# Attention backward on one core: a new written-out order of loads, stores and units, copies moved between ScalarE and VectorE

## The chip, the cores and the metric

The kernel runs on one core of a Trainium2 chip. The metric is the device time of one launch in microseconds; the median of eleven runs before the change is 672.09 us (670.6 to 673.2).

## What is computed

The reference is a grouped-query softmax attention together with its gradients: 32 batches, 32 query heads that share 4 key and value heads, 4 query rows per head, 2048 keys, depth 128, all bfloat16.

```python
B, Hq, Hkv, Sq, Sk, D = 32, 32, 4, 4, 2048, 128
k = jnp.repeat(k, Hq // Hkv, axis=1)
v = jnp.repeat(v, Hq // Hkv, axis=1)
p = softmax(einsum("bhqd,bhkd->bhqk", q, k) * D ** -0.5)
out = einsum("bhqk,bhkd->bhqd", p, v)
# returned: out, and the gradients dq, dk, dv for a given grad_out
```

For one batch there are 4 key heads with 8 x 4 = 32 query rows each, so the 128 query rows fill the 128 partitions exactly. K and V of a batch are 4 MB and are read once; dK and dV of a batch are 4 MB and are written once.

## The kernel before, in words

Nothing is looped over in the usual sense. The string PLAN (line 28) is cut into pieces of four characters, each piece a unit of work: its kind, its part, a PSUM bank or slot or engine, and a tile number. `plan()` (line 149) turns it into a list of 3232 units, and the loop at line 323 emits them in that order inside a manual schedule. An engine executes its instructions in the order in which they were emitted, so PLAN sets the order on each engine and on SyncE, which issues every DMA. What binds different engines to each other are the data, the PSUM banks and the SBUF tiles that are used again.

The units, by the names that `emit` (line 214 on) uses:

- LK and LV load half of a batch's K or V, two heads, as one row of 8192 bytes per partition in one of 20 slots (`slots`, line 189). The K rows carry q or grad_out as 256 further bytes. The DMA is issued on SyncE at line 226. For batch 0 each load is cut in two at column 2048.
- KT and VT transpose K and V on TensorE, four blocks of 128x128 in fp32 pairs (line 241); KTe, VTe copy them from PSUM to SBUF, on ScalarE (line 207) or on VectorE (line 209) by the letter A or D in the plan. QT and QTe do the same for q and grad_out (line 230 and lines 207 or 209), ET and DT for the probabilities and for dS.
- S is Q K^T in PSUM (line 255), MX the row minimum on VectorE (line 260), EX the exponential on ScalarE (line 264), RC the reciprocal of the sum (line 268). DP is dO V^T (line 255 too) and DS the product for the softmax gradient on VectorE (line 303).
- dop, qp and rs are scalings on GpSimd (lines 271 to 278). O and DQ are the products with V and K (line 288), Oe and DQe their scaled copies (line 294 on ScalarE, line 296 on VectorE), which go into the last 128 columns of an output row.
- DV and DK compute one quarter of the keys for two heads, into two PSUM banks (line 310); DVe and DKe copy these 128x1024 numbers as bfloat16 into an output row (line 316), on ScalarE or VectorE. `heads_of` (line 212) splits the row in two heads, so that a copy writes two pieces of 512.
- SV and SK store a finished output row of dV or dK (line 320).

Loads and outputs share the 20 slots. A load into a slot that held an output row waits until that row's store has landed; a load into a slot that held K or V waits for the last reader. DMAs use eight semaphores in turn, and each waits until the DMA eight places ahead of it has landed, so at most eight are in flight. In the middle of the plan every batch issues in the order LV1, LK0, SK1, SV1, LV0, SV0, LK1, SK0, with each load belonging to a batch three or four later than the one in work. `unpaired` (line 332) puts the output columns into the reference's order on the host; it is not part of the time.

Of the kernel before, what the change touches and what calls it, by code (L numbers as in the profile page):

```python
# [14 lines left out]
P = 128  # L15
# [6 lines left out]

NAMES = dict(
# [5 lines left out]
    "a000a110b120a030b040a150e400f4A0e011f0A0e702f7A0e513f5A0b160a070e224f2A0e135f1D0c000d0D0e316f3A0g720h7A0e637f6A0"  # L29
    "b080a190g601h6D0g212h2A0i040i1-0j0D0g303h3A0e411f4A0e024f0A0g104h1D0k0A0g415h4D0g026h0D0l0D0e705f7A0e516p020q0A0"  # L30
    "f5D0b1a0p131q1D0m0-0A340B3A0A060B0D0A100B1A0a0d0r020r1-0s0D0t0D0o0-0A640B6A0A760B7D0u020v0D0g502h5A0A540B5A0E1c0"
    "b0e0A460B4A0e210f2D0e102f1D0c020d0D0e333f3A0A240B2A0E0b0u160v1D0g703h7A0e617f6A0n0-0C020D0D0C140D1A0C360D3D0a1h0"
    "g604h6A0g216h2A0i021i1-0j0D0C200D2A0g360h3A0e470f4A0w100x1A0k0A0g111h1D0g462h4D0g075h0D0C400D4D0w061x0A0l0D0e072"
    "f0A0C620D6A0F0f0C740D7D0e763f7A0e504p010q0A0f5D0b1i0p171q1D0m0-0A320B3A0A040B0D0A100B1A0a040r060r1-0s0D0t0D0A720"
    "B7D0o0-0A640B6A0u061v0D0g500h5A0y010C540D5A0y1-0z0D0F1g0A520B5A0E120b0c0A460e201f2A0B4D0e115f1D0c040d0D0e356f3A0"
    "A220B2A0E0j0u160v1D0g701h7A0e617f6A0n0-0C040D0D0C120D1A0C360D3D0a180g605h6A0g216h2A0i020i1-0j0D0C200D2A0g360h3A0"
    "e471f4A0w101x1A0g112h1D0k0A0g463h4D0g074h0D0C400D4D0w060x0A0l0D0e072f0A0C620D6A0F060C740D7D0e765f7A0e506p010q0A0"
    "f5D0b100p171q1D0m0-0A320B3A0A040B0D0A100B1A0a0g0r060r1-0s0D0t0D0o0-0A620B6A0A740B7D0y070C500D5A0y1-0z0D0F1b0u020"
    "v0D0g560h5A0A540B5A0E1f0b020A400B4D0e270f2A0e163f1A0c020d0D0e334f3D0A240B2A0E010u100v1D0g722h7A0e637f6A0n0-0C060"
    "D0D0C140D1A0C300D3D0a130g624h6A0g236h2A0i041i1-0j0D0C220D2A0g300h3A0C720e410f4A0w100x1A0g111h1D0k0A0g403h4D0g015"  # L40
    "h0D0C440D4A0w001x0D0l0D0D7A0e012f0D0C660D6A0F0a0e743f7D0e504p020q0A0f5D0b150p111q1D0m0-0A340B3A0A060B0D0A120B1A0"
    "a0b0r000r1-0s0D0t0D0o0-0A640B6A0A760B7D0y010C520D5A0y1-0z0D0F1j0u041v0D0g500h5A0A560B5A0E160b0f0A420B4D0e211f2A0"
    "e105f1A0c040d0D0e356f3D0A260B2A0E0e0u120v1D0g711h7A0e607f6A0n0-0C040D0D0C160D1A0C320D3D0a170g615h6A0g206h2A0i040"
    "i1-0j0D0C200D2A0g320h3A0e431f4A0w101x1A0g112h1D0k0A0g423h4D0g034h0D0C400D4D0w020x0A0l0D0e032f0A0C640D6A0F0i0C760"
    "D7D0e725f7A0e506p010q0A0f5D0b190p131q1D0m0-0A340B3A0A060B0D0A100B1A0a0j0r020r1-0s0D0t0D0o0-0A640B6A0A760B7D0y030"
    "C500D5A0y1-0z0D0F110u040v0D0g520h5A0A560B5A0E1a0b060A400B4D0e230f2A0e123f1A0c040d0D0e354f3D0A260B2A0E0c0u100v1D0"
    "g732h7A0e627f6A0n0-0C040D0D0C160D1A0C300D3D0a1h0g634h6A0g226h2A0i041i1-0j0D0C220D2A0g300h3A0e410f4A0w120x1A0g131"
    "h1D0k0A0g403h4D0g015h0D0C420D4D0w001x0A0l0D0e012f0A0C640D6A0F000C760D7D0e703f7A0e514p020q0A0f5D0b1e0p131q1D0m0-0"
    "A340B3A0A060B0D0A100B1A0a010r020r1-0s0D0t0D0o0-0A640B6A0A760B7D0y030C500D5A0y1-0z0D0F1d0u041v0D0g520h5A0A560B5A0"
    "E1i0b0a0A400B4D0e231f2A0e125f1A0c040d0D0e356f3D0A260B2A0E020u100v1D0g731h7A0e627f6A0n0-0C040D0D0C160D1A0C300D3D0"  # L50
    "a180g635h6A0g226h2A0i040i1-0j0D0C220D2A0g300h3A0e411f4A0w121x1A0g132h1D0k0A0g403h4D0g014h0D0C420D4D0w000x0A0l0D0"
    "e012f0A0C640D6A0F050C760D7D0e705f7A0e516p020q0A0f5D0b1f0p131q1D0m0-0A340B3A0A060B0D0A100B1A0a0d0r020r1-0s0D0t0D0"
    "o0-0A640B6A0A760B7D0y030C500D5A0y1-0z0D0F140u040v0D0g520h5A0A560B5A0E100b090A400B4D0e230f2A0e123f1A0c040d0D0e354"
    "f3D0A260B2A0E0c0u100v1D0g732h7A0e627f6A0n0-0C040D0D0C160D1A0C300D3D0a1g0g634h6A0g226h2A0i041i1-0j0D0C220D2A0g300"
    "h3A0e410f4A0w120x1A0g131h1D0k0A0g403h4D0g015h0D0C420D4D0w001x0A0l0D0e012f0A0C640D6A0F0i0C760D7D0e703f7A0e514p020"
    "q0A0f5D0b160p131q1D0m0-0A340B3A0A060B0D0A100B1A0a040r020r1-0s0D0t0D0o0-0A640B6A0A760B7D0y030C500D5A0y1-0z0D0F130"
    "u041v0D0g520h5A0A560B5A0E150b0e0A400B4D0e231f2A0e125f1A0c040d0D0e356f3D0A260B2A0E020u100v1D0g731h7A0e627f6A0n0-0"
    "C040D0D0C160D1A0C300D3D0a1b0g635h6A0g226h2A0i040i1-0j0D0C220D2A0g300h3A0e411f4A0w121x1A0g132h1D0k0A0g403h4D0g014"
    "h0D0C420D4D0w000x0A0l0D0e012f0A0C640D6A0F000C760D7D0e705f7A0e516p020q0A0f5D0b1a0p131q1D0m0-0A340B3A0A060B0D0A100"
    "B1A0a030r020r1-0s0D0t0D0o0-0A640B6A0A760B7D0y030C500D5A0y1-0z0D0F170u040v0D0g520h5A0A560B5A0E1i0b0f0A400B4D0e230"  # L60
    "f2A0e123f1A0c040d0D0e354f3D0A260B2A0E0c0u100v1D0g732h7A0e627f6A0n0-0C040D0D0C160D1A0C300D3D0a190g634h6A0g226h2A0"
    "i041i1-0j0D0C220D2A0g300h3A0e410f4A0w120x1A0g131h1D0k0A0g403h4D0g015h0D0C420D4D0w001x0A0l0D0e012f0A0C640D6A0F0h0"
    "C760D7D0e703f7A0e514p020q0A0f5D0b150p131q1D0m0-0A340B3A0A060B0D0A100B1A0a070r020r1-0s0D0t0D0o0-0A640B6A0A760B7D0"
    "y030C500D5A0y1-0z0D0F1j0u041v0D0g520h5A0A560B5A0E100b060A400B4D0e231f2A0e125f1A0c040d0D0e356f3D0A260B2A0E020u100"
    "v1D0g731h7A0e627f6A0n0-0C040D0D0C160D1A0C300D3D0a1e0g635h6A0g226h2A0i040i1-0j0D0C220D2A0g300h3A0e411f4A0w121x1A0"
    "g132h1D0k0A0g403h4D0g014h0D0C420D4D0w000x0A0l0D0e012f0A0C640D6A0F010C760D7D0e705f7A0e516p020q0A0f5D0b1i0p131q1D0"
    "m0-0A340B3A0A060B0D0A100B1A0a0j0r020r1-0s0D0t0D0o0-0A640B6A0A760B7D0y030C500D5A0y1-0z0D0F180u040v0D0g520h5A0A560"
    "B5A0E1h0b0a0A400B4D0e230f2A0e123f1A0c040d0D0e354f3D0A260B2A0E0c0u100v1D0g732h7A0e627f6A0n0-0C040D0D0C160D1A0C300"
    "D3D0a1f0g634h6A0g226h2A0i041i1-0j0D0C220D2A0g300h3A0e410f4A0w120x1A0g131h1D0k0A0g403h4D0g015h0D0C420D4D0w001x0A0"
    "l0D0e012f0A0C640D6A0F0d0C760D7D0e703f7A0e514p020q0A0f5D0b100p131q1D0m0-0A340B3A0A060B0D0A100B1A0a080r020r1-0s0D0"  # L70
    "t0D0o0-0A640B6A0A760B7D0y030C500D5A0y1-0z0D0F1g0u041v0D0g520h5A0A560B5A0E110b050A400B4D0e231f2A0e125f1A0c040d0D0"
    "e356f3D0A260B2A0E020u100v1D0g731h7A0e627f6A0n0-0C040D0D0C160D1A0C300D3D0a160g635h6A0g226h2A0i040i1-0j0D0C220D2A0"
    "g300h3A0e411f4A0w121x1A0g132h1D0k0A0g403h4D0g014h0D0C420D4D0w000x0A0l0D0e012f0A0C640D6A0F040C760D7D0e705f7A0e516"
    "p020q0A0f5D0b1h0p131q1D0m0-0A340B3A0A060B0D0A100B1A0a0g0r020r1-0s0D0t0D0o0-0A640B6A0A760B7D0y030C500D5A0y1-0z0D0"
    "F1b0u040v0D0g520h5A0A560B5A0E1d0b0i0A400B4D0e230f2A0e123f1A0c040d0D0e354f3D0A260B2A0E0c0u100v1D0g732h7A0e627f6A0"
    "n0-0C040D0D0C160D1A0C300D3D0a1a0g634h6A0g226h2A0i041i1-0j0D0C220D2A0g300h3A0e410f4A0w120x1A0g131h1D0k0A0g403h4D0"
    "g015h0D0C420D4D0w001x0A0l0D0e012f0A0C640D6A0F030C760D7D0e703f7A0e514p020q0A0f5D0b110p131q1D0m0-0A340B3A0A060B0D0"
    "A100B1A0a0b0r020r1-0s0D0t0D0o0-0A640B6A0A760B7D0y030C500D5A0y1-0z0D0F190u041v0D0g520h5A0A560B5A0E140b000A400B4D0"
    "e231f2A0e125f1A0c040d0D0e356f3D0A260B2A0E020u100v1D0g731h7A0e627f6A0n0-0C040D0D0C160D1A0C300D3D0a150g635h6A0g226"
    "h2A0i040i1-0j0D0C220D2A0g300h3A0e411f4A0w121x1A0g132h1D0k0A0g403h4D0g014h0D0C420D4D0w000x0A0l0D0e012f0A0C640D6A0"  # L80
    "F070C760D7D0e705f7A0e516p020q0A0f5D0b1d0p131q1D0m0-0A340B3A0A060B0D0A100B1A0a090r020r1-0s0D0t0D0o0-0A640B6A0A760"
    "B7D0y030C500D5A0y1-0z0D0F1e0u040v0D0g520h5A0A560B5A0E130b0h0A400B4D0e230f2A0e123f1A0c040d0D0e354f3D0A260B2A0E0c0"
    "u100v1D0g732h7A0e627f6A0n0-0C040D0D0C160D1A0C300D3D0a1i0g634h6A0g226h2A0i041i1-0j0D0C220D2A0g300h3A0e410f4A0w120"
    "x1A0g131h1D0k0A0g403h4D0g015h0D0C420D4D0w001x0A0l0D0e012f0A0C640D6A0F0f0C760D7D0e703f7A0e514p020q0A0f5D0b140p131"
# [64 lines left out]
def plan():  # L149
    text, seen, units = "".join(PLAN), collections.Counter(), []  # L150
    for at in range(0, len(text), 4):
        key = text[at:at + 2]
        u = Unit()
        u.name, u.part, u.b = NAMES[key[0]], int(key[1]), seen[key]
        u.where, u.tile = text[at + 2], int(text[at + 3], 36)
        seen[key] += 1
        units.append(u)
# [3 lines left out]
def kernel(  # L161
# [160 lines left out]
    with tc.manual_schedule():  # L322
        for u in units:
            emit(u)
# [37 lines left out]
```

## Time and profile before

| | before |
|---|---|
| median of 11 runs, us | 672.09 |
| the profiled execution's own time, us | 672.05 |
| its span, us | 670.1 |
| mean granted TensorE clock | 0.986 |
| PE busy, us | 606.2 |
| VectorE busy, us | 571.8 |
| ScalarE busy, us | 569.4 |
| bytes moved by DMA, MB | 273.96 |
| mean rate over the span, GB/s | 409 |
| output copies of line 316: on ScalarE | 292 of 1023 ns |
| output copies of line 316: on VectorE | 220 of 1218 ns |
| copies of transposes: on ScalarE | 445 of about 600 ns (512 fp32 words wide) |
| copies of transposes: on VectorE | 195 of about 685 ns |
| median time from a load's or store's issue to its landing, us | 17.8 to 20.5 |

The span runs from the first to the last instruction of the profiled execution; its own time has 1.95 us more around it. A page of the profile divides the span in 40 slices and gives for each the busy share of the engines in tenths, the mean busy share of the 16 DMA engines, and the rate. A busy share is an average over stages: a wait matters only where it ends last. Three engines and the DMA queue are all busy for 85% of the span or more, so the reading has to go stretch by stretch.

### The profile page before, as it was taken

Reading aid. Unit: us, or ns where it says so; the run is one execution under the profiler, and the core shown is the slowest. Engines: PE = TensorE matmul, PEld = TensorE weight load, DVE = VectorE, ACT = ScalarE, POOL = GpSimd, SP = SyncE. Lnnn points to the kernel's source line nnn. Section 1 sums busy time; section 2 is a strip of 40 time slices with the busy share of each in tenths; the row PEclk is TensorE's granted clock in tenths of the full one; section 3 lists DMA queues with packets and bytes.
Section 4 is the critical chain, followed back from the end, with each engine's and each line's share of the span. In section 5 each row is a group of like instructions: output and inputs, shape, how many; then the busy total and the mean of one; then the engine's idle time right before and its main releaser. Section 6 shows DMA issues by size and latency. Waiting matters only on the chain.

```text
span 670.1 us, 20678 instructions
## 1 busy us (share of the span) xinstructions
PE 606.2 (90%) x8768; PEld 399.4 (60%) x8768; DVE 571.8 (85%) x736; ACT 569.4 (85%) x802; POOL 39.0 (6%) x102
## 2 busy tenths in 40 slices
PE   5998999999998999988998989888999988898994
PEld 5665666666665666655666656555565665565652
DVE  1988799999997999988898889887988988887893
ACT  3997899999997899988898889887888988887894
POOL 0000000000000000000000000000000000000000
PEclk9999899999998999999999999998999999999997
DMA  8999999999999999999999999999999999999967
GB/s 347 421 424 422 418 376 423 423 423 424 423 424 425 424 425 422 423 427 426 422 422 407 408 414 423 423 426 416 393 421 416 421 421 408 410 421 425 375 245 314
DMA packets 37532, 273.96 MB, mean 409 GB/s; under 512 B 4160, under 2 KB 4160, under 8 KB 5184
## 3 DMA queue, kind: packets, MB, share of 16 engines
q1 hardware_dynamic: 37440, 272.65, 98.2%
q8 instruction: 68, 1.11, 0.6%
q14 instruction: 24, 0.20, 0.1%
HBM read 136.31 MB, written 136.31 MB: 407 GB/s over the span
## 4 chain that ended last, share of the span: by engine, by line
DMA 47%; PE 40%; ACT 4%; DVE 4%; issue 3%; SPq 0%; POOL 0%; DVEq 0%; ACTq 0%; POOLq 0%
DMA row<-in_k_dram 47%; PE psum L241 20%; PE psum L310 9%; PE psum L288 6%; PE psum L255 5%; ACT row L316 3%; DVE vt_sb L209 3%; DVE ds_sb L303 1%; DVE row L316 0%; ACT e_sb L264 0%; DVE e_sb L260 0%; PE psum L230 0%; ACT dt_sb L207 0%; SPq L226 0%; DVE row L296 0%
## 5 line engine op out<-in xcount | busy, mean ns | idle before, releaser
L316 ACT CAST row<-psum 128x1024 bf16<-128x1024 f32 x292 | 289.2, 1023 | 30.8 <-PE psum L310 28.5
L241 PE MATMUL psum<-ident,row 128*128 128x128 f32 x2048 | 287.6, 282 | 30.1 <-DMA row<-in_k_dram 23.9
L241 PEld LDWEIGHTS psum<-ident,row 128*128 128x128 f32 x2048 | 222.7, 142 | 96.7 <-issue 30.6
L316 DVE CAST row<-psum 128x1024 bf16<-128x1024 f32 x220 | 264.9, 1218 | 5.6 <-PE psum L310 2.6
L207 ACT COPY kt_sb<-psum 128x512 f32<-128x512 f32 x190 | 110.1, 599 | 22.3 <-PE psum L241 22.2
L207 ACT COPY vt_sb<-psum 128x512 f32<-128x512 f32 x160 | 92.0, 602 | 34.1 <-PE psum L241 33.5
L303 DVE SCALAR_TENSOR_TENSOR ds_sb<-psum,delta,e_sb 128x1024 bf16<-128x1024 f32 x64 | 82.1, 1283 | 12.9 <-PE psum L255 8.3
L310 PE MATMUL psum<-ds_sb,qp_sb 32*128 32x512 bf16 x512 | 77.3, 385 | 3.4 <-ACT row L316 1.0
L260 DVE TENSOR_SCALAR_CACHE_REDUCE e_sb<-psum 128x2048 bf16<-128x2048 f32 x32 | 73.3, 2292 | 5.7 <-PE psum L255 5.7
L310 PE MATMUL psum<-e_sb,dop_sb 32*128 32x512 bf16 x512 | 68.4, 387 | 2.4 <-issue 0.9
L209 DVE COPY vt_sb<-psum 128x1024 bf16<-128x1024 bf16 x96 | 60.7, 685 | 10.1 <-PE psum L241 9.9
L209 DVE COPY kt_sb<-psum 128x1024 bf16<-128x1024 bf16 x66 | 45.0, 684 | 28.6 <-PE psum L241 27.8
L264 ACT ACTIVATE e_sb<-psum,m 128x2048 bf16<-128x2048 f32 x32 | 64.0, 2001 | 0.2 <-DVE e_sb L260 0.2
L271 POOL TENSOR_SCALAR dop_sb<-row,rinv 128x128 bf16<-128x128 bf16 x32 | 19.3, 603 | 603.4 <-DVE rinv L268 585.2
L241 PE MATMUL psum<-ident,ds_sb 128*128 128x128 f32 x256 | 42.2, 288 | 9.6 <-DVE vt_sb L209 7.0
L288 PE MATMUL psum<-row,dt_sb 128*32 128x128 bf16 x2048 | 44.0, 224 | 5.4 <-issue 5.3
L310 PEld LDWEIGHTS <-qp_sb 32*128 32x128 bf16 x512 | 19.4, 91 | 46.3 <-issue 42.9
L255 PE MATMUL psum<-vt_sb,qdt_sb 128*32 128x512 bf16 x512 | 40.7, 388 | 4.3 <-issue 4.3
L288 PEld LDWEIGHTS <-dt_sb 128*32 128x32 bf16 x2048 | 31.2, 96 | 21.6 <-issue 20.9
L241 PEld LDWEIGHTS psum<-ident,ds_sb 128*128 128x128 f32 x256 | 27.1, 141 | 27.2 <-DVE vt_sb L209 16.4
L207 ACT COPY dt_sb<-psum 128x512 f32<-128x512 f32 x63 | 38.4, 610 | 1.0 <-PE psum L241 0.9
L288 PEld LDWEIGHTS <-et_sb 128*32 128x32 bf16 x2048 | 31.0, 96 | 13.8 <-ACT et_sb L207 11.3
(29 smaller groups left out, 308.5 us busy)
## 6 DMA issues: line engine op xcount, KB each, us to landing
out_dram<-row SPq DMA_DIRECT2D x64, 1056.0 KB, 20.0
out_dram<-row SPq DMA_DIRECT2D x64, 1024.0 KB, 20.4
row<-in_k_dram SPq DMA_DIRECT2D x62, 1056.0 KB, 17.8
row<-in_v_dram SPq DMA_DIRECT2D x62, 1024.0 KB, 20.5
row<-in_v_dram SPq DMA_DIRECT2D x4, 512.0 KB, 9.8
row<-in_k_dram SPq DMA_DIRECT2D x2, 544.0 KB, 5.6
row<-in_k_dram SPq DMA_DIRECT2D x2, 512.0 KB, 4.4
```

What stands on the lines that cost most here:

```text
L207: nc.scalar.copy(out=out.bitcast(FP32), in_=in_)
L209: nc.vector.tensor_copy(out=out, in_=in_.bitcast(BF16))
L241: nc.tensor.transpose(out=ps[:, P * j:P * j + P], in_=src[:, 4 * half + j, :], identity=ident32[:])
L255: nc.tensor.matmul(out[r, QW * w:QW * w + QW], lhsT=t["qdt"][:, P * side + 32 * h:P * side + 32 * h + 32], rhs=t[x, NH * i + h][:, QW * w: ...
L260: nc.vector.tensor_scalar(out=t["e"][:], in0=t["S"], scalar1=-scale, scalar2=None, op0=ALU.mult, op1=ALU.min, accum_out=t["m"][:])
L264: nc.scalar.activation(out=t["e"][:], in_=t["S"], func=ACT.Exp, bias=t["m"][:], scale=scale, accum_out=t["l"][:])
L271: nc.gpsimd.tensor_scalar(out=t["dop"][:], in0=t["go"], scalar1=t["rinv"][:], scalar2=None, op0=ALU.mult)
L288: nc.tensor.matmul(t[name][r, :], lhsT=left[:, j, r, odd], rhs=right[:, 4 * i + j, :, odd], start=(i == 0 and c == 0), stop=(i == 1 and c ...
L303: nc.vector.scalar_tensor_tensor(out=t["ds"][:, w], in0=t["DP", i], scalar=t["dl"][:], in1=t["e"][:, w], op0=ALU.subtract, op1=ALU.mult)
L310: nc.tensor.matmul(acc[:, QW * (h % 2):QW * (h % 2) + QW], lhsT=t[still][rows[h], :], rhs=t[moving][rows[h], QW * i:QW * i + QW], start=Tr ...
L316: copy(out=heads_of(t[name[:2], "out", g])[:, :, QW * i:QW * i + QW], in_=t[name[:2], i, g].rearrange("p (h c) -> p h c", h=2))
```

## The change

PLAN is replaced as a whole: 3236 units instead of 3232. The bytes moved and the matrix products are the same. What is different in the order and in the code:

- In the middle of the plan the four loads of a batch stand together, ahead of the stores SK0 of the previous batch and SV0, SV1, SK1. The first twelve loads stand ahead of the first store. In the last five batches loads and stores are mixed irregularly.
- Units on TensorE stand at other places relative to each other and use other PSUM banks.
- Copies change their engine. On ScalarE there are now 345 output copies (from 292), 314 copies of transposes (from 445), 30 of the 32 copies QTe (from none) and 30 of the 64 scaled copies Oe and DQe (from none); VectorE has the rest.
- The loads of batch 0 are no longer cut in two. The four stores of batch 31 are cut in two halves instead, by parts 2 to 5 of SV and SK.
- An output copy writes 1024 neighbouring columns of the row instead of two pieces of 512, and `unpaired` undoes this.
- Ahead of the first unit TensorE does 20 transposes of the identity into the last PSUM bank.

```diff
+LAST = 31
+WARM_UP = 20
...
         u.name, u.part, u.b = NAMES[key[0]], int(key[1]), seen[key]
+        if u.name in ("SV", "SK") and u.part > 1:
+            u.b = LAST
...
-            T[u.b]["D" + u.name[1], "out", u.part] = slots[int(u.where, 36)]
+            T[u.b]["D" + u.name[1], "out", u.part % 2] = slots[int(u.where, 36)]
...
-            for w in (slice(0, Sk), slice(Sk, n)) if b == 0 else (slice(0, n),):
-                nc.sync.dma_start(out=x[:, w], in_=src[:, w])
+            nc.sync.dma_start(out=x[:, 0:n], in_=src)
...
-            copy(out=heads_of(t[name[:2], "out", g])[:, :, QW * i:QW * i + QW],
-                 in_=t[name[:2], i, g].rearrange("p (h c) -> p h c", h=2))
+            copy(out=t[name[:2], "out", g][:, 2 * QW * i:2 * QW * i + 2 * QW], in_=t[name[:2], i, g])
         elif name in ("SV", "SK"):
-            n = LONG if i else ROW
-            nc.sync.dma_start(out=(dv_r if name == "SV" else dk_r)[i][b], in_=t["D" + name[1], "out", i][:, 0:n])
+            half, g = divmod(i, 2)
+            n = LONG if g else ROW
+            w = (slice(0, n), slice(0, ROW // 2), slice(ROW // 2, n))[half]
+            nc.sync.dma_start(out=(dv_r if name == "SV" else dk_r)[g][b][:, w], in_=t["D" + name[1], "out", g][:, w])
...
+        for _ in range(WARM_UP):
+            nc.tensor.transpose(out=psum[:, QW * (BANKS - 1):QW * (BANKS - 1) + P], in_=ident32[:], identity=ident32[:])
...
-    return x.reshape(2, 32, P, 2, 8, P, 2).transpose(1, 0, 3, 5, 4, 6, 2).reshape(32, NH, 16 * P, P)
+    return x.reshape(2, 32, P, 4, 2, 2, P, 2).transpose(1, 0, 4, 6, 3, 5, 7, 2).reshape(32, NH, 16 * P, P)
```

The plan itself is some 120 lines of such text. In readable form, the DMAs of a middle batch and the S, O and QT units between which they stand (the number after the dot is the batch) are:

```diff
- S.16  SK0.15  LV1.18  LK0.19  O.16  SK1.15  SV1.16  LV0.18  QT.17  SV0.16  LK1.19  S.17
+ S.17  LK0.19  LV1.19  LK1.19  LV0.19  SK0.16  O.17  SV0.16  QT.18  SV1.16  SK1.16  S.18
```

From the last load on the two plans go on like this:

```diff
- LV0.31 QT.30 SV0.29 S.30 SK0.29 O.30 SK1.29 SV1.30 QT.31 SV0.30 S.31 SK0.30 O.31 SK1.30 SV1.31 SV0.31 SK0.31 SK1.31
+ LV0.31 SK0.28 SK0.29 O.30 SV0.29 QT.31 SV1.29 S.31 SV0.30 SK1.29 SV1.30 SK0.30 O.31 SV2.31 SK1.30 SV3.31 SK2.31 SK3.31 SV4.31 SV5.31 SK4.31 SK5.31
```

## The prediction

> **What bounds the kernel now.** I read the page's slices and queue table first, then the busy times of single stretches, then SyncE's own timeline of issues. In the page's 40 slices the DMA row and the rate row are the flat ones:
>
> ```profile
> PE   5998999999998999988998989888999988898994
> DMA  8999999999999999999999999999999999999967
> GB/s 347 421 424 422 418 376 423 423 423 424 423 424 425 424 425 422 423 427 426 422 422 407 408 414 423 423 426 416 393 421 416 421 421 408 410 421 425 375 245 314
> q1 hardware_dynamic: 37440, 272.65, 98.2%
> ```
>
> Each slice is 16.75 us. Nearly all stand at 421 to 427 GB/s; the sag is at the first slice, at slice 6, in the second half in places, and in the last three. The stretches show whether a sag is an empty queue (DMA share under 1) or slower packets (share 1, fewer GB/s). The columns are the busy us of PE, PEld, DVE, ACT and POOL, then the clock, the DMA share and GB/s:
>
> ```profile
> 140.00:150.00 10.00, 9.96 (x202) 6.15 (x200) 9.33 (x15) 9.25 (x14) 0.59 (x2) 1.00 1.01 424
> 570.00:580.00 10.00, 9.88 (x125) 6.20 (x124) 9.25 (x10) 8.89 (x14) 0.00 (x0) 1.00 1.02 413
> 630.00:640.00 10.00, 9.10 (x182) 5.57 (x169) 8.32 (x12) 8.27 (x12) 0.00 (x0) 1.00 0.85 347
> 640.00:650.00 10.00, 9.24 (x136) 5.86 (x134) 9.46 (x12) 9.45 (x14) 1.20 (x3) 1.00 0.49 199
> 650.00:660.00 10.00, 8.83 (x150) 4.43 (x147) 8.69 (x11) 9.30 (x12) 0.00 (x0) 0.89 0.85 346
> ```
>
> So the queue is full to about 630 us and empties after it. SyncE's timeline says why: the last load goes out at 618.78, and the eleven stores behind it are spread over 41 us, each waiting for its evictions.
>
> ```profile
> 618.78 0.34 SPq L226 DMA_DIRECT2D row<-in_v_dram  x1
> 621.21 41.27 SPq L320 DMA_DIRECT2D out_dram<-row  x11
> ```
>
> Compute is not far behind: between 90 and 200 us the chain's repeating pieces (the S matmuls at 94.39, 113.31, 132.37, 151.22) come every 18.9 us. A batch moves 272.65 MB/32 = 8.52 MB, which at 423 GB/s takes 20.1 us. PE's 18.9 us is hidden as long as the queue is full; loads run ahead only until the 20 slots are used up.
>
> **A budget of the profiled execution** (span 670.1 us, own time 672.05, so 1.95 lie around it; the median of the eleven runs, 672.09, is the same). First data at about 2.0 us (the stretch 1 to 2 us moved 66 GB/s). All 273.96 MB at 423 GB/s: 647.7. Empty queue in the tail: (423-347)/423 of 10 us, and the same for 199 and 346, is 1.8 + 5.3 + 1.8 = 8.9. From the last data (rate zero from about 666.1) to the span's end: 4.0. Sum 662.6; the other 7.5 are about 1.1 of slow start (292 GB/s over the first 10 us is 3.1 less than full, 2.0 of it the lead), 2.1 between 80 and 100 us (371 and 387 GB/s), and 4.3 of slower packets after 350 us.
>
> **What the Trainium skill says.** "HBM Reference", Specifications: a core that streams alone reaches about 425 GB/s, limited by its 16 DMA engines. The trace agrees: 426 GB/s where only loads run (10 to 20 us) and 424 where loads and stores alternate, so sorting them by direction has no rate to win beyond this. "DMA: Bandwidth & Descriptors", Latency and other measured facts, puts most of a DMA's fixed cost into the receipt of its write; here 4.0 us pass after the last data, which the change keeps. "TensorE: Matmul & The Clock Gate", What's actually happening: the array starts at half clock until it has been busy for some 3.4 us. The trace agrees: the first 8 transposes take 1.94 us, later ones 1.02 to 1.1. Price: "ScalarE: Activation LUTs", What ACT_TABLE_LOAD costs, gives 186 ns + 0.833 ns per element for an ACTIVATE with immediates, 93 ns more for each pointer operand (512 wide: 612 estimated, 599 to 610 measured).
>
> **The change, part by part.**
>
> *Order of loads and stores.* Bytes are unchanged, so the 647.7 us stay. What can move is the empty queue. Counting in the two plans, at the S of a middle batch before has issued 10 loads from this batch's own on and owes 2 stores of earlier batches; after has 8 and 4. At S of batches 30 and 31 before has 8 and 4 loads, 2 and 2 stores; after 4 and 4 loads, 7 and 5 stores. Behind the very last load stand 11 stores in before (11.7 MB) and in after 9 whole and 8 half ones, worth 13: 13.8 MB or 33 us of queue. The compute that then remains: in before, from the V transposes of batch 31 (about 639 us) to the last eviction (662.1) 23 us. So V of batch 31 lands 33 us before the end of data and compute needs about 23 to 25: the queue can stay full. I keep 1.5 us of the 8.9, since margins are a few us: saving 7.4.
>
> *Waits this adds.* Loads queue on SyncE in a group behind the last store of an earlier batch, and that store waits for its copies; everything behind waits too. Besides, a load that refills a store's slot now stands 5 to 7 places behind that store (33 of 51 such loads); in before 7 (27), 9 to 11 (6) or 13 (21). At 5 places four transfers of 2.5 us are behind the awaited one: 10 us of cover, against about 2.3 us from landing to new data (1.3 from the first issue at 0.72 to data at 2.0, about 1 for the signal). So nothing is lost in a full queue; without that cover a load costs 2.3. Two loads have distance 2 (one of them K of batch 31), cover 2.5: about zero, counted in the tail's 1.5. In the first 60 us the first store stands behind 12 loads (12.5 MB, full to 31 us) and is ready at about 26, but the next stores depend on batch 1's second half: bounds 0 and 5 us of empty queue, I take 1. In exchange the loss of 2.1 at 80 to 100 us, which I lay to the old order without proof, goes.
>
> *Copies moved.* ACT: 292 to 345 output copies, +53 x 1023 = +54.2 us; transposes' copies 445 to 314, -131 x 600 = -78.6; 30 qdt copies (128 wide, est. 293 ns by the price) +8.8; 30 scaled copies of O and DQ (est. 386 ns) +11.6: -4.0 us of 569. DVE: -53 x 1218, +131 x 685, -30 x 281, -30 x 346 = +6.3 of 572. Per batch 17.7 and 18.1 us, under PE's 18.9 and the queue's 20.1: counted as zero. Without the queue's cover it would be 0.2 us per batch on DVE.
>
> *Units moved singly.* PE's sum is the same 606 us. That PE keeps 18.9 us in the new order the trace can't show; up to 20.1 it costs nothing (bound below: nothing, as the queue sets the pace; above: the rival).
>
> *Output rows contiguous.* Same elements per copy; 0, bounds -0.1 to +0.1 us on a 1.0 to 1.2 us copy, hidden like the rest.
>
> *First loads whole, last stores in halves.* Four DMAs fewer at the start (4 x 0.4 us of issue), four more at the end. The 512 KB loads ran at 372 GB/s between 6 and 8 us; whole ones win back about 0.6 of the slow start. The final store is 0.54 instead of 1.08 MB and waits alone for DQ, worth up to 1.3 us, already inside the tail's 1.5.
>
> *Warm-up.* 20 transposes at 1.94/8 = 0.24 us are 4.8 us, from 1.6 to 6.4; the first K row, now 1.05 MB, lands at about 5.9. PE loses 0.5 and then finds a full clock; compute starts some 2 us sooner (S of batch 0 at 14.93 before). DMA doesn't follow: 0.
>
> Sum: 2.0 + 647.7 + 0.5 start + 1.0 early gaps + 4.0 slow packets (the cause isn't visible, so kept) + 1.5 tail + 4.0 = 660.7; with 1.95 around it **662.6 us**.
>
> **Rivals.**
> - *Slow packets vanish too* (their dips recur every 20 us with the old order's phase; but 100 to 340 us had that order without dips): no early gap and tail 0, 656.7.
> - *The tail's gap stays*, because batch 31's compute is as late as before: 2.0 + 647.7 + 0.5 + 4.3 + 2.1 + 8.9 + 4.0 + 1.95 = 671.4. Against it: the stores owed.
> - *Slower: the queue runs dry once in every batch*, at the last store before the group of loads on SyncE, since its copies come late with only four transfers behind. Price: the gap at 83 to 85 us (shares 0.68 and 0.78) is 0.54 us; 29 batches are 15.7, 662.6 + 15.7 = 678.3. It decides from (672.1 - 662.6)/29 = 0.33 us per batch. PE falling past 20.7 us per batch would look alike in time. Against it: 10 us of cover.
>
> **Numbers.** 0.2% (1.3 us) is about what a measurement here can tell from no change. Main case 0.50 (faster), packets gone 0.22 (faster), tail stays 0.11 (0.04 faster, 0.05 same, 0.02 slower), dry queue 0.17 (0.01 faster, 0.01 same, 0.15 slower). Faster 0.77, same 0.06, slower 0.17. The range runs from 656 (no gap at all) to 674 (tail stays, early gaps of 5 us in part): it leaves out nearly all of the dry queue.
>
> **What would show it.** Right: the last three slices at 400 or more, DMA share near 1 until some 5 us before the end, S every 20.1 to 20.4 us in the middle, the first S near 12 us. Wrong: shares under 0.95 in every period, PE waiting for loads or ACT and DVE for slots at a period over 20.5, or a middle rate away from 423.

## The result and the profile after

The kernel after takes 676.75 us (12 runs, 675.1 to 680.42), the kernel before 672.55 (46 runs, 670.6 to 674.84): a ratio of 1.0068, with a 95% interval of 1.0058 to 1.0079. It is slower by 4.2 us, where 662.6 was forecast. The profiled execution of after took 676.08 us with a span of 673.8, 3.7 more than the 670.1 before.

The page of the kernel after, the rows that were read of before:

```profile
PE   8998999999998999999799999999989899999986
DMA  9999999999999999999999999999999989998998
GB/s 367 411 421 426 419 373 409 422 424 424 424 407 404 420 390 424 424 425 389 353 423 423 425 421 426 423 424 424 425 419 414 423 344 383 423 424 328 385 422 326
q1 hardware_dynamic: 37440, 272.65, 98.2%
```

The sag of the last slices is gone but for its edges: slices 38 and 39 ran at 385 and 422 GB/s, where before had 375 and 245 (the forecast had all of the last three at 400 or more; the last has 326). In its place there are new sags in the middle, at slices 12, 13, 15, 19, 20, 33, 34 and 37. Single stretches of after (us of PE, PEld, DVE, ACT, POOL; clock; DMA share; GB/s) show of which kind they are:

```profile
140.00:150.00 10.00, 10.00 (x201) 6.52 (x200) 9.40 (x14) 9.02 (x14) 0.40 (x2) 1.00 1.01 425
320.00:330.00 10.00, 7.13 (x109) 4.47 (x108) 7.02 (x11) 5.70 (x8) 1.20 (x3) 1.00 0.89 302
550.00:560.00 10.00, 9.63 (x136) 6.29 (x136) 9.25 (x15) 9.61 (x15) 1.20 (x3) 1.00 0.74 270
570.00:580.00 10.00, 9.71 (x168) 6.03 (x170) 9.87 (x15) 9.97 (x14) 1.20 (x3) 1.00 1.01 423
620.00:630.00 10.00, 8.88 (x133) 6.03 (x133) 8.21 (x9) 8.62 (x13) 0.00 (x0) 1.00 0.76 243
630.00:640.00 10.00, 10.00 (x146) 6.74 (x146) 9.77 (x14) 8.97 (x14) 1.22 (x3) 1.00 1.01 423
640.00:650.00 10.00, 8.46 (x140) 4.75 (x136) 7.58 (x9) 9.04 (x13) 0.85 (x2) 1.00 1.01 423
650.00:660.00 10.00, 9.18 (x184) 5.53 (x177) 6.79 (x11) 9.35 (x13) 0.37 (x1) 1.00 1.01 419
```

The kernel before in three of these stretches (the others stand in the prediction):

```profile
320.00:330.00 10.00, 9.04 (x192) 5.58 (x187) 8.35 (x12) 7.98 (x11) 0.00 (x0) 1.00 1.02 424
550.00:560.00 10.00, 9.88 (x99) 6.12 (x88) 9.41 (x9) 8.89 (x15) 0.00 (x0) 1.00 1.02 406
620.00:630.00 10.00, 9.69 (x110) 6.75 (x111) 9.62 (x13) 9.38 (x15) 1.20 (x3) 1.00 0.99 416
```

At 630 to 660 us the queue is full, with 419 to 423 GB/s where before moved 347, 199 and 346. At 320, 550 and 620 the DMA share is 0.74 to 0.89, before 0.99 to 1.02: the queue was empty there for part of the time. At 550 PE, DVE and ACT are busy for 9.3 to 9.6 of the 10 us all the same: there the queue waits for compute. SyncE's own timeline of after has the last load ten microseconds later than before, and 17 stores behind it where there were 11:

```profile
628.88 0.67 SPq L229 DMA_DIRECT2D row<-in_v_dram  x1
632.01 37.15 SPq L324 DMA_DIRECT2D out_dram<-row  x17
```

The chain of work that ended last, by engine, in before and then in after, and three pieces of it in after, the S matmuls between 92 and 132 us:

```profile
DMA 47%; PE 40%; ACT 4%; DVE 4%; issue 3%; SPq 0%; POOL 0%; DVEq 0%; ACTq 0%; POOLq 0%
PE 60%; DMA 18%; ACT 11%; DVE 6%; issue 3%; SPq 0%; POOL 0%; DVEq 0%; ACTq 0%; POOLq 0%
```
```profile
92.76 0.98 PE psum L258 x16
112.30 0.98 PE psum L258 x16
131.84 1.01 PE psum L258 x16
```

The largest share has passed from DMA to PE. The S matmuls come every 19.5 us in this stretch; before they came every 18.9 there.

How much transfer time was lost, and when: the rate of each 20 us stretch, taken as (424 - rate)/424 x 20 us and summed up to the time at the head of the column.

| us lost up to | 100 | 260 | 340 | 540 | 620 | 640 | 660 |
|---|---|---|---|---|---|---|---|
| before | 5.3 | 5.5 | 5.5 | 9.5 | 10.8 | 12.7 | 19.9 |
| after | 5.0 | 8.7 | 12.8 | 13.4 | 19.3 | 23.6 | 23.8 |

The last 20 us gained what was forecast, and the rest gave it back with 3.9 us on top. That is the whole difference of the two spans (3.7).

The pace, in us: when S of batch 0, 9, 16, 24 and 31 is finished, taken as the start of MX, which reads it (some 1.1 to 1.4 us after the first matmul of S), and then the span. S9 stands for batch 9. Four kernels of the experiments stand with them:

| | S0 | S9 | S16 | S24 | S31 | end |
|---|---|---|---|---|---|---|
| before | 16.0 | 191.2 | 332.6 | 497.6 | 641.8 | 670.1 |
| after | 12.2 | 192.3 | 343.5 | 504.7 | 641.8 | 673.8 |
| before, a quarter of the transfers (q1) | 14.8 | 186.7 | 319.3 | 470.8 | 603.8 | 628.0 |
| after, a quarter of the transfers (q2) | 11.8 | 193.1 | 333.4 | 492.0 | 625.4 | 655.3 |
| old plan, new code (w1) | 13.8 | 190.5 | 330.5 | 495.6 | 640.8 | 668.5 |
| after, one hole closed (e1) | 12.3 | 192.3 | 340.4 | 505.7 | 642.2 | 674.4 |

S of batch 31 is finished at the same time before and after; what follows takes 28.3 us before and 32.0 after.

### The profile page after: what moved, and what is told of

Read it like the earlier page. It is cut to its first block, busy times and chain, and to the rows that moved or that the text cites. A ratio compares the mean times of both kernels' runs of the same rounds, so it can differ in the third digit from the quotient of the medians.

```text
span 673.8 us, 20678 instructions
## 1 busy us (share of the span) xinstructions
PE 628.9 (93%) x8788; PEld 416.0 (62%) x8788; DVE 577.3 (86%) x754; ACT 572.1 (85%) x784; POOL 39.1 (6%) x102
## 4 chain that ended last, share of the span: by engine, by line
PE 60%; DMA 18%; ACT 11%; DVE 6%; issue 3%; SPq 0%; POOL 0%; DVEq 0%; ACTq 0%; POOLq 0%
PE psum L244 32%; DMA out_dram<-row 14%; PE psum L313 13%; PE psum L291 7%; ACT row L319 7%; PE psum L258 7%; DMA row<-in_v_dram 4%; DVE vt_sb L214 2%; DVE row L319 1%; ACT vt_sb L212 1%; ACT kt_sb L212 1%; DVE e_sb L263 1%; ACT e_sb L267 1%; PE psum L328 1%; DVE kt_sb L214 1%
## 5 line engine op out<-in xcount | busy, mean ns | idle before, releaser
L319 ACT CAST row<-psum 128x1024 bf16<-128x1024 f32 x345 | 340.3, 1024 | 38.9 <-PE psum L313 28.7
L244 PE MATMUL psum<-ident,row 128*128 128x128 f32 x2048 | 291.1, 283 | 14.1 <-DVE vt_sb L214 6.6
L319 DVE CAST row<-psum 128x1024 bf16<-128x1024 f32 x167 | 202.8, 1218 | 17.8 <-PE psum L313 11.3
L214 DVE COPY kt_sb<-psum 128x1024 bf16<-128x1024 bf16 x167 | 114.3, 687 | 27.9 <-PE psum L244 17.8
L313 PE MATMUL psum<-ds_sb,qp_sb 32*128 32x512 bf16 x512 | 90.3, 388 | 13.7 <-ACT row L319 8.1
L214 DVE COPY vt_sb<-psum 128x1024 bf16<-128x1024 bf16 x121 | 80.5, 686 | 10.1 <-PE psum L244 7.7
L212 ACT COPY vt_sb<-psum 128x512 f32<-128x512 f32 x135 | 77.4, 600 | 9.4 <-PE psum L244 9.0
L212 ACT COPY kt_sb<-psum 128x512 f32<-128x512 f32 x89 | 52.0, 601 | 15.3 <-PE psum L244 14.2
L313 PEld LDWEIGHTS <-dop_sb 32*128 32x128 bf16 x512 | 22.2, 91 | 39.5 <-issue 28.7
L244 PE MATMUL psum<-ident,e_sb 128*128 128x128 f32 x256 | 39.4, 280 | 0.1
L258 PEld LDWEIGHTS <-qdt_sb 128*32 128x32 bf16 x1024 | 20.8, 95 | 27.3 <-issue 20.5
## 6 DMA issues: line engine op xcount, KB each, us to landing
out_dram<-row SPq DMA_DIRECT2D x62, 1056.0 KB, 13.4
out_dram<-row SPq DMA_DIRECT2D x62, 1024.0 KB, 13.4
```

Source lines behind the costliest of these rows:

```text
L212: nc.scalar.copy(out=out.bitcast(FP32), in_=in_)
L214: nc.vector.tensor_copy(out=out, in_=in_.bitcast(BF16))
L244: nc.tensor.transpose(out=ps[:, P * j:P * j + P], in_=src[:, 4 * half + j, :], identity=ident32[:])
L258: nc.tensor.matmul(out[r, QW * w:QW * w + QW], lhsT=t["qdt"][:, P * side + 32 * h:P * side + 32 * h + 32], rhs=t[x, NH * i + h][:, QW * w: ...
L313: nc.tensor.matmul(acc[:, QW * (h % 2):QW * (h % 2) + QW], lhsT=t[still][rows[h], :], rhs=t[moving][rows[h], QW * i:QW * i + QW], start=Tr ...
L319: copy(out=t[name[:2], "out", g][:, 2 * QW * i:2 * QW * i + 2 * QW], in_=t[name[:2], i, g])
```

## The experiments

Two theories stood at first. **Theory A**: the new order on SyncE makes holes, since loads stand close behind the stores whose slots they need, or behind stores that are not ready. **Theory B**: the new order of the units sets a slower pace on the engines.

### Closing the holes of the queue

In the trace of after, LK1.17 (the load of the second K row of batch 17) is issued at 320.28, when the store two places ahead, whose slot it takes, has landed at 320.26. LK0.28 stands behind SK0.25, which is not ready before 553.25. In the last batches two loads stand 2 to 4 places behind the stores that free their slots. Each was mended alone, then all three (loads and stores in SyncE's order, with slots):

```diff
e1 - SV0.13@13 SV1.13@15 LK1.17@13 SK1.13 LK0.17 LV1.17 LV0.17 SK0.14
e1 + SV0.13@13 SV1.13@15 SK1.13 LK0.17 LV1.17 LV0.17 LK1.17@13 SK0.14
e2 - LK1.28 SK0.25 LK0.28 LK0.29
e2 + LK1.28 LK0.28 SK0.25 LK0.29
e3 - LK1.30 SK0.27 LK0.30 SV0.27@f SV1.27 SV1.28 LK1.31 SK1.27@0 LV0.30 LK0.31@0
e3 + LK1.30 SV0.27@f SV1.27 SK0.27 LK0.30 SV1.28 LK1.31 SK1.27@0 LV0.30 LK0.31@f
```

> The changed kernel with one load moved: K1 of batch 17, which stands two places behind the store that frees its slot, goes behind V0 of batch 17. Theory A (SyncE's order leaves too little behind a waiting instruction, and every hole in the queue is lost for good): the hole between 318 and 326 us (about 4 us under 423 GB/s) goes, the time falls from 676.75 by 2.5 to 4.5 us to 672 to 674. Theory B (the new order of units on the engines sets the pace, 19.5 us per batch, and the queue only follows): within 1 us of 676.75.

> The changed kernel with K0 of batch 28 moved ahead of SK0 of batch 25, directly behind K1 of batch 28. Its slot is long free. Theory A: the hole between 550 and 562 us (about 4 us) shrinks by one transfer, 1.5 to 3.5 us less, 673 to 675. Theory B: within 1 us of 676.75.

> The changed kernel with SV0 and SV1 of batch 27 issued directly behind K1 of batch 30, and slots exchanged so that K0 of batch 31 no longer waits for SK1 of batch 27 two places ahead of it. Theory A: the hole between 616 and 630 us (5.3 us) goes, 3 to 5.5 us less, 671 to 674. Theory B: the end is set by the units left after the last S, not by the queue: within 1 us of 676.75.

> The three moves together. Theory A: the gains add, 8 to 13 us less, 664 to 669, faster than before. Theory B: within 2 us of 676.75. A mixed case, in which a later hole opens for each one closed, would give 670 to 675.

Measured: e1 675.92, e2 676.11, e3 680.66, all three 680.12 (ratios to before 1.0056, 1.0058, 1.0129 and 1.0103). In e1 the hole did close: 426 and 419 GB/s at 300 to 340 us, where after had 396 and 364, and S16 is finished 3 us sooner. But by S24 it is 1 us behind after again (table above). In e2 the hole shrank (372 GB/s at 540 to 560 us, after 338), and the time did not follow. Single holes aren't the cause of the loss: closing one brings 0.8 us at most, which is within the spread of after's own runs. The other two edits test nothing of this, because they put two stores ahead of LK0.30. In e3 that load lands at 614.68 instead of 608.30, and TensorE waits for it, which it doesn't in after (e4 likewise, 3.33 us):

```profile
614.81 0.63 PE L253 MATMUL psum<-ident,row 128*128 128x128 f32 x4 [3.36 <-DMA row<-in_k_dram]
```

What SyncE waited for in the whole run says more than single holes do (us in total, times, the longest), before and then after:

```profile
SPq L320 <- DMA out_dram<-row: 121.6, 62, 2.3
SPq L226 <- DMA out_dram<-row: 102.5, 23, 5.6
SPq L320 <- DVE row L316: 91.6, 15, 9.5
SPq L226 <- DMA row<-in_v_dram: 79.1, 41, 2.1
```
```profile
SPq L324 <- ACT row L297: 144.7, 22, 13.4
SPq L324 <- DVE row L319: 122.8, 35, 11.8
SPq L324 <- ACT row L319: 105.2, 45, 8.2
SPq L229 <- DMA out_dram<-row: 104.1, 28, 14.8
```

Loads that wait for the store of their slot (L226, L229) cost SyncE as much before as after, 102.5 and 104.1 us. But before, most of the other waits (254 us) are for the landing eight places ahead, so the next transfer was ready and the queue full; in after these are 19 us. For the copies that fill a row to be stored, SyncE waits 388 us in after and 188 in before: the queue has lost its lead over compute. Whether that is because the stores stand at other places or because the units are slower, this view can't tell.

### The units alone

Kernels before and after with a quarter of each transfer (a slot's first load is whole), all units, banks and copies kept. The edit in after (in before the same lines):

```diff
-            nc.sync.dma_start(out=x[:, 0:n], in_=src)
+            w = slice(3 * ROW // 4 if u.where in used else 0, n)
+            used.add(u.where)
+            nc.sync.dma_start(out=x[:, w], in_=src[:, w])
...
-            w = (slice(0, n), slice(0, ROW // 2), slice(ROW // 2, n))[half]
+            w = (slice(3 * ROW // 4, n), slice(ROW // 4, ROW // 2), slice(3 * ROW // 4, n))[half]
+            used.add(u.where)
```

> The kernel before with DMAs cut: after a slot's first use its loads bring only the last quarter of the row (with q or grad_out), and all stores write only the last quarter, so most of K and V is stale and three quarters of dK and dV are left out. All engine work stays. It measures the compute pace alone. Both theories: 18.9 us per batch as between 90 and 200 us, about 16 + 31 x 18.9 + 28 = 630 us.

> The changed kernel with the same cut of loads and stores. Theory B (the new order of units is slower by itself): 19.5 us per batch and a longer end, 12 + 31 x 19.5 + 32 = 648 us, 15 to 20 us over the kernel before cut likewise. Theory A (only the queue makes the difference): 18.9 us per batch or less, no more than 5 us over it.

Measured: 630.79 and 657.43 (two runs each, 1 and 0.3 us around that). With the transfers out of the way the new order is 26.6 us slower, more than theory B had put on it (18). By the table above 15 us of it arise between S9 and S31, 9 before them and 6 behind S31, while S of batch 0 is done 3 us sooner. A long middle stretch, q1 and then q2:

```profile
320.00:510.00 190.00, 185.80 (x2747) 122.70 (x2746) 179.50 (x231) 176.54 (x252) 11.97 (x30) 1.00 0.39 119
```
```profile
320.00:515.00 195.00, 189.60 (x2723) 125.27 (x2722) 179.39 (x237) 174.34 (x237) 11.69 (x30) 1.00 0.38 115
```

From S16 to S24 a batch takes 18.9 us in q1 and 19.8 in q2. DVE and ACT are busy for 94% and 93% of the stretch in q1, and for 92% and 89% in q2: the two engines that copy are no fuller than before.

### The code without the plan

> The plan of before with the code of after: 20 warm-up transposes, whole first loads, contiguous output rows, no halved stores. Both theories lay the loss to the plan: 670.5 to 672.5. If the code parts cost something themselves: over 674.

The edit to the kernel after; the warm-up, the whole first loads and the contiguous output rows stay:

```diff
-PLAN = (the 3236 units of after)
+PLAN = (the 3232 units of before)
```

Measured: 670.12, ratio 0.9966 (0.9954 to 0.9978). So the code gains about 2 us and the plan loses some 6.6. Of the kernels that do the whole work, none is faster.

### Old units with the new queue, and the reverse

The units of one plan and the loads and stores of the other, merged in the order in which each became possible; the slots had to be given out anew. A middle batch, as in the list of the change, first before and x1, then after and x2:

```diff
- S.16  SK0.15  LV1.18  LK0.19  O.16  SK1.15  SV1.16  LV0.18  QT.17  SV0.16  LK1.19  S.17
+ S.17  LK0.19  LV1.19  LK1.19  LV0.19  SK0.16  SV0.16  O.17  SV1.16  SK1.16  QT.18  S.18
- S.17  LK0.19  LV1.19  LK1.19  LV0.19  SK0.16  O.17  SV0.16  QT.18  SV1.16  SK1.16  S.18
+ S.17  SV0.16  LK1.19  O.17  SK0.16  LV1.19  LK0.20  QT.18  SK1.16  SV1.17  LV0.19  S.18
```

> The units of TensorE, VectorE, ScalarE and GpSimd in the order of before, with its banks and engines; the loads and stores on SyncE in the order of after (groups of four, halves at the end), and the code of after. Slots are given out anew, with at least 6 places between a store and the load into its slot and at least 5 between a store and the copies into its slot. If the loss lies in the order of the units (theory B), this is no slower than the kernel with the whole old plan and the new code (670.1): 664 to 671. If grouping the loads and stores itself loses (theory A in another form), 673 to 680.

> The counterpart: units of after, loads and stores in the order of before, the code of after; slots given out anew, at least 6 places between a store and what fills its slot next. Theory B: the loss is here too, 674 to 681. If the grouping of loads and stores makes the loss: 668 to 672.

Measured: 685.09 (1.018, 1.0144 to 1.0217) and 715.63 (1.0645, 1.063 to 1.0659). Both are far above what either theory had said. In x1 output copies stand behind stores; a group of its page shows the idle time of DVE before them and whose work ended most of it:

```profile
L319 DVE CAST row<-psum 128x1024 bf16<-128x1024 f32 x220 | 265.2, 1219 | 30.1 <-DMA out_dram<-row 19.7
```

In x2 loads come too late, and DMA has 76% of its chain. As merged here, each order of the queue does harm with the units of the other plan; both hybrids have slots of their own besides, so the loss can't be split between units and queue by exchanging them. The new units do 39 us better with the grouping (after) than with the old queue (x2), so the grouping isn't shown to be bad in itself.

### Where TensorE waits

I set the matmuls of the trace beside the units of the plan, and for each unit took the time from the end of the copy that last emptied its bank (for units of two banks also the second bank and matmul) to its start. Units that waited stand out, since they start 50 to 57 ns after that copy. Over middle batches, of 42 units per batch:

| | mean us per batch | units that start within 66 ns of their bank's release |
|---|---|---|
| q1, before | 18.96 | 6.0 |
| q2, after | 19.82 | 11.9 |
| before, whole transfers | | 6.7 |
| after, whole transfers | | 11.4 |

The time inside units grows from 10.00 to 10.31 us per batch, that between units from 8.96 to 9.51: together the 0.86 us of the table. (Of the time between, what lies above the shortest switch seen for the same pair of kinds goes from 2.58 to 3.33, the rest from 6.38 to 6.18; this split depends on which pairs are taken together.) New in after are waits of DK7 for the copy of KT0 (0.30 us), of DK4's second half for that of VT0 (0.28), of DK5 for that of DV0 (0.28) and, in nearly half of the batches, of DV5 for that of DK5 (0.21 as a mean). One such place, PE and then ACT in q2:

```profile
397.06 0.60 PE L246 MATMUL psum<-ident,ds_sb 128*128 128x128 f32 x4
397.60 0.69 PE L315 MATMUL psum<-ds_sb,qp_sb 32*128 32x512 bf16 x4
398.22 0.44 PE L246 MATMUL psum<-ident,e_sb 128*128 128x128 f32 x2
```
```profile
397.26 0.59 ACT L212 COPY kt_sb<-psum 128x512 f32<-128x512 f32 x1 [0.45 <-PE psum L246]
```

The four matmuls of DK6 and DK7 take 0.69 us: DK7 starts at 397.90, 51 ns after the copy of KT0, which ended at 397.85. The same two units in q1 take 0.39 us, with all four matmuls within 10 ns of each other on four row groups:

```profile
380.28 0.66 PE L242 MATMUL psum<-ident,row 128*128 128x128 f32 x4
380.87 0.39 PE L311 MATMUL psum<-ds_sb,qp_sb 32*128 32x512 bf16 x4
381.20 0.98 PE L242 MATMUL psum<-ident,row 128*128 128x128 f32 x7
```

PE counts as busy for nearly all of such a wait, so no row for PE's idle time shows it. PE's busy time does: over the same matrix products it is 599.4 us in q1 and 624.2 in q2, the warm-up of 4.5 included. **Theory B1**: these waits for banks make the pace. **B2**: TensorE's own sequence is longer. **B3**: the copies are the pace anyway, and a wait that is taken away comes back elsewhere.

### Shorter output copies

```diff
-            copy(out=t[name[:2], "out", g][:, 2 * QW * i:2 * QW * i + 2 * QW], in_=t[name[:2], i, g])
+            copy(out=t[name[:2], "out", g][:, 2 * QW * i:2 * QW * i + QW].rearrange("p (h c) -> p h c", h=2),
+                 in_=t[name[:2], i, g].rearrange("p (h c) -> p h c", h=2)[:, :, 0:QW // 2])
```

> The kernel before with a quarter of each transfer (as in the earlier run of this kind, 630.8 us) and with the copies of the dV and dK units to half width: every copy still reads both of its banks, but moves 512 of 1024 elements for each partition, so half of dV and dK is left out, and a bank of such a unit comes free some 0.4 to 0.6 us sooner. Theory B1 (the units wait for a bank whose copy is late): below 612. Theory B2 (TensorE's own sequence is the limit, with its switches and row groups): 626 to 631.

> The same two cuts in the kernel after (657.4 us with the quarter of the transfers alone). B1: the distance to the kernel before, 26.6 us with whole copies, falls to under 10 us, since the switches between kinds of units cost after no more than before. B2: the distance stays at 20 to 28 us.

Measured: 622.68 and 638.81. The distance falls from 26.6 to 16.1 us, between the two expectations, and the units that wait from 6.0 to 4.0 and from 11.9 to 7.4 per batch. Some 10 us of the loss hung on output copies. DK7 still waits 0.30 us for KT0, and DK4's second half now 0.58 for VT0: those banks are emptied by copies of transposes, which were left whole. q3 itself lies between the two theories too. So this neither separates B1 from B2 nor settles B3.

### One bank, exchanged both ways

Only bank numbers are edited (b is the first bank of a unit). In after, for 21 batches (y2 with a quarter of the transfers, y1 with all; every other batch has b2 and b3 for b0 and b1, two have other numbers), and in before, for 26 batches (z1, a quarter):

```diff
y - KT0 b0  DT0 b4  DK6 b6  DK7 b0  ET0 b5  KT7 b4
y + KT0 b0  DT0 b1  DK6 b6  DK7 b4  ET0 b0  KT7 b4
z - DT0 b0  KT0 b1  DK6 b4  DK7 b6  KT7 b0  KT5 b1
z + DT0 b0  KT0 b1  DK6 b4  DK7 b0  KT7 b6  KT5 b7
```

> The kernel after with a quarter of each transfer (657.4 us before this edit). Only banks are exchanged, in 21 batches, and no unit or copy is moved: DK7 no longer takes the bank that KT0 has just filled, but the free pair that DT0 and ET0 used, and these two take single banks freed earlier. In the trace DK7 starts 51 ns after KT0's copy ends, some 0.3 us after DK6, where in the kernel before the two start together. Theory B1 (such waits for banks make the pace): 21 x 0.30 = 6.3 us less, 651; at least 3 of it stays if KT7, which now follows DK7's copy, waits a little. Theory B3 (the copies' throughput is the pace, and a wait that is removed comes back at the next unit): 656 to 658.

> The reverse in the kernel before with a quarter of each transfer (630.8 us): in 26 batches DK7 is put on the pair of banks that DT0 and KT0 have just filled, and KT7 and KT5 take the pair it had. No unit or copy is moved. B1: DK7 waits for KT0's copy as it does in after, 26 x 0.30 = 7.8 us more, 638.6, with 5 to 9 more as bounds. B3: 630 to 632.

> The kernel after with all its transfers and the exchange of banks of the quarter run. B1: PE's pace of 19.5 us per batch falls to 19.2 in 21 batches; with the queue of transfers taking about 20.1 per batch in the middle, only part of 6.3 us shows in the time: 671 to 675. B3: 676 to 677.

Measured: z1 651.87, against 630.79. One unit per batch on the wrong bank, with two that change places with it, costs before 21 us; an undisturbed middle batch goes from 18.85 to 19.57 us, about that of after. PE and ACT of z1 at the place:

```profile
397.99 0.66 PE L242 MATMUL psum<-ident,row 128*128 128x128 f32 x4
398.58 0.54 PE L311 MATMUL psum<-ds_sb,qp_sb 32*128 32x512 bf16 x3
399.32 0.37 PE L311 MATMUL psum<-ds_sb,qp_sb 32*128 32x512 bf16 x1 [0.20 <-ACT kt_sb L207]
```
```profile
398.69 0.58 ACT L207 COPY kt_sb<-psum 128x512 f32<-128x512 f32 x1
```

The last matmul of DK7 starts 50 ns after the copy of KT0 ended (399.27). The copy takes 0.6 us and is not late; it is simply asked for at once. The wait is 0.73 us (0.16 of it for the copy of DT0, the rest for KT0's) rather than the 0.30 that I had taken over from after; over 26 batches that explains 19 of the 21. In z1's trace stand besides five stops of TensorE of 1.7 to 2.1 us, of the kind that h1 shows below; q1 has none. B1 is shown as a sufficient cause: order, engines and copies are those of before, and the time comes within 6 us of after's units. The length of the waits counts and not their number: z1 has 8.0 waiting units per batch, after 11 to 12.

The other way gains less. y2 takes 654.22, 3.2 of the 6.3 us at stake: the wait of DK7 is gone, but KT7 now waits 0.12 us for DK7's copy, and DK5's wait grows by 0.08. Some 12 units per batch still wait, no fewer than without the edit. Here B3 holds for half. y1 takes 676.54, no change: under whole transfers a wait less in the middle is worth nothing, which B3 had said and B1 had not.

### A little room

After takes some 19 us more with whole transfers than its units alone, and neither closing holes nor taking a wait away moved it. **Theory C**: units (655.3 us of span) and transfers (660.7 by the prediction's budget) are so near each other that every delay on one side is passed on and not made up. The edit to the quarter runs, in before and after alike:

```diff
-            w = slice(3 * ROW // 4 if u.where in used else 0, n)
+            w = slice(ROW // 8 if u.where in used else 0, n)
```

> The kernel before with all its units and seven eighths of each transfer (a slot that is filled again, and each store, leaves out the first eighth of its row). At 424 GB/s the transfers then take about 567 us, and the units alone 630.8. Theories C and A both: 630 to 636.

> The same cut in the kernel after, whose units alone take 657.4. Theory C (whole transfers take about as long as the units of after, and with neither ahead of the other every short delay of one is passed on to the other and is not made up): one eighth of room is enough, and the time falls from 676.75 to 656 to 661. Theory A, in the form that is left (the place of the stores ahead of the groups of loads makes holes whatever the room): 665 or more.

Measured: h2 660.0. One eighth of room brings after to 2.6 us above its units alone (spans 657.4 and 655.3): theory C, and once more not A. h1 took 655.82, 20 us and more above what both had said. Most of its batches keep 18.8 to 18.9 us, but about every seventh takes 22.5 to 24. The timeline of PE in h1 at one of these:

```profile
321.63 0.66 PE L242 MATMUL psum<-ident,row 128*128 128x128 f32 x4
322.22 0.39 PE L311 MATMUL psum<-e_sb,dop_sb 32*128 32x512 bf16 x2
325.31 0.39 PE L311 MATMUL psum<-e_sb,dop_sb 32*128 32x512 bf16 x2 [2.70 <-issue]
```

PE waits for nothing that the profile shows. But the queue for instructions brings packets of 16 KB, two for each batch, and one of them ran from 323.05 to 323.93. Of h1's stops of over 1.4 us after the first 40 us, all eight end 1.2 to 1.5 us after the end of such a packet; together they are 20.5 us, and the clock was halved for 3.4 us after five of them. So h1 most likely waited for its own program, and its distance to 630.8 is not a limit of its units. Two packets that follow each other closely are 3.3 to 5 us apart in q1, which has no stop of this size, and seldom under 6 in h1. That would fit a fetch that stands behind data on its DMA engine. But z1, with a quarter of the transfers and packets as close as in q1, has five stops that end 1.2 to 1.5 us after such a packet, so data on the DMA engines is not needed for them, and why a fetch comes late stays open.

### What can be kept

```diff
- SK1.30 SV1.31 SV0.31 SK0.31 SK1.31
+ SV3.31 SK1.30 SV5.31 SV2.31 SV4.31 SK3.31 SK2.31 SK4.31 SK5.31
```

> The old plan with the new code (670.1), and the stores of the last batch in halves as in after, the first halves as soon as their copies are out. Theory B: the last store is half as long, 1.3 us, and its first half no longer waits for the last units: 668 to 670. If the tail is limited by when the units end: 670, no change.

Measured: 670.53, ratio 0.9972 (0.9963 to 0.9981): no different from w1. The halved stores bring nothing that can be measured.

## Why the prediction was wrong, point by point

**"I keep 1.5 us of the 8.9 ... saving 7.4"** was right where it looked. From 640 us on, after loses 0.2 us of transfer. But the lost time was not taken away, it was moved: 10.2 us go between 540 and 640, where before lost 3.2, in part to a queue that waits for compute. In the terms of the sum: the lead, the start, the early gaps, the slow packets and the tail made 9.0 us of lost transfer time, and after lost 23.8 up to 660 us. These 14.8 us more hold the whole miss of 14.1 (676.75 against 662.6).

**"That PE keeps 18.9 us in the new order the trace can't show; up to 20.1 it costs nothing"** is the step that failed, in both halves. PE does not keep 18.9: it needs 19.5 in the quickest stretches and 19.8 from S16 to S24 (q2), because the new order and its banks make 11 to 12 units per batch wait for a copy where 6 did. The order of copies and banks was in the plans to be read, and I costed "units moved singly" only by PE's sum of busy time. And "up to 20.1 it costs nothing" compared two middle periods, though what counts are the whole lengths: the units alone take 655.3 us from end to end, with a third batch of 23.9 us (before 20.2) and 29.9 us after S31 (before 24.2). The budget for the transfers was 660.7. Before had 628.0 against 670.1, and could make up a delay at 1.2 us per batch (20.1 - 18.9); after makes up 0.3 to 0.6. That the plan loses and not the code is shown (w1), and so are the slower units (q1, q2), a wait for a bank as a sufficient cause (z1), and the lack of room (h2). How the loss of the whole divides between the units and the places of loads and stores is not, nor how much each of the waits takes of it.

**"Waits this adds ... 10 us of cover"** was wrong in size. Transfers took 13 to 15 us from issue to landing in after, and each of the 14 loads that stand two to five places behind their slot's store went out only when that store had landed; LK1.17 at two places did stop the queue. The "about 1 for the signal" stood on no trace; LK1.17 was issued 0.02 us after the landing. Yet e1 shows that this stop was not the cause, and the waits for slots are no longer in sum than before. "So nothing is lost in a full queue" failed by its premise: the queue was not kept full, since SyncE waited for copies twice as long as before.

**"1.0 early gaps" and "4.0 slow packets"** were both off. The slow packets that the prediction kept did vanish: after loses 0.6 us between 340 and 540, before 4.0. But 7.8 us of sags came between 100 and 340, where before lost 0.2 and the prediction put nothing. The loss at 80 to 100 us, which I had laid to the old order without proof, stayed: 380 GB/s again.

**Copies moved**: forecast -4.0 us on ACT and +6.3 on DVE, measured +2.7 (569.4 to 572.1) and +5.5 (571.8 to 577.3). "Counted as zero" was wrong for another reason: what counts is not the sum of the copies' time but when a copy empties its bank.

**Warm-up, first loads, contiguous rows**: "some 2 us sooner" was too little. The first matmul of S of batch 0 starts at 10.79 us, where before had 14.93 and the forecast was near 12; with the old plan and the same code (w1) it starts at 12.7. Copies into contiguous rows take 1024 and 1218 ns, as before. What the code brings alone (w1) is 2.1 us beside before in its own comparison (672.18); the sum had given it 0.6, at the start.

**The rival that was nearest** is the slower one. Its queue did run dry behind stores that waited for copies, though not once in every batch, and one sentence of it named the other half: "PE falling past 20.7 us per batch would look alike in time". PE fell to 19.5 to 19.8, and with transfers of nearly the same length that was enough. The sum of the rival without slow packets is off by half a microsecond: its terms make 656.2, not 656.7.

The Trainium skill says in "Perfetto Trace Analysis", Matmuls, that independent matmul groups should rotate through different PSUM banks, so that the evacuation of one overlaps the next group. The traces agree and give it a price here: with all eight banks in use in both plans, one choice of which is next cost z1 some 19 us beside q1's 631.

## What to carry to other kernels

Two plans with the same products and nearly the same copies can differ by when a bank comes free: list for each unit the copy that empties its bank, and count what stands between the two, before calling a reordering free. Compare the units' length from end to end with that of the transfers, not one middle period with another: here units of 655.3 us and transfers of some 660.7 took 673.8 together, and an eighth less of transfer took 657.4. And try an order of the queue with the order of the units that it was made for: exchanging one alone, with slots given out anew, cost 15 to 45 us beside the old plan with the same code.

## What the runs showed of the hardware

- A unit that waits for a bank starts 50 to 57 ns after the end of the copy that frees it.
- Neighbouring DV or DK units on different row groups start 3 to 4 ns apart (DK6 and DK7 in q1); when one has to wait, the pair takes 0.69 us and not 0.39.
- Eight stops of TensorE in h1 (1.4 to 3.9 us) end 1.2 to 1.5 us after the end of an instruction packet; with the halved clock after it, such a stop makes a batch some 4.5 us longer. That the packet is what TensorE waits for is inferred from these times. The Trainium skill, "Runtime: NRT & Kernel Launch", Instruction fetch mechanics, calls the cost of crossing a 16 KiB boundary "mostly hidden". In q1 it is hidden (no such stop), in h1 it is not, nor in z1 (five stops, with a quarter of the transfers). With whole transfers, 4 of before's 15 stops of this size end like that.
